# One scale per block of 256 columns of the three input matrices, from the sum of all squares: top-k attention with a maxout layer

## Chip, cores and metric

The kernel runs on one core of a Trainium2 chip. The metric is the device time of one execution in microseconds (us). The time before is 1222.91 us, the median of three runs (1222.42 to 1224.28).

## Reference

Attention over 8 batches with 8 heads, 576 positions and 64 columns a head keeps in each row of scores the 32 largest and takes the softmax of these alone. The rows of all heads, 512 wide, then go through a maxout layer: the largest of three products with 512 x 768 matrices, and a product with a 768 x 512 matrix.

```python
scores = scale * np.matmul(q, k.transpose(0, 1, 3, 2))
kth = np.partition(scores, -top_k, axis=-1)[..., -top_k:-top_k + 1]
scores = np.where(scores >= kth, scores, -1000000000.0)
...
attn = attn / (np.sum(attn, axis=-1, keepdims=True) + 1e-09)
x = np.matmul(attn, v)
...
h = np.maximum(np.maximum(x @ w1, x @ w2), x @ w3)
return h @ w_out
```

Inputs and output are float32; the kernel gets the weights as the low and high words of 64-bit numbers.

## The kernel before

**Attention.** A unit is a batch, one pair of heads and one or two blocks of 128 rows; the last 64 rows of two pairs of heads make one unit of their own. TensorE multiplies q and k (qk, L469), ScalarE brings the scores to SBUF (evac, L477), VectorE finds the largest of seven stretches of each row (sweep, L486) and from them a pivot; ScalarE marks what lies above the pivot (sign, L526), GpSimd multiplies (window, L531), VectorE takes the eight largest of the rest and picks the 32nd (below, L535, and pick), and masks the row (mask, L574). ScalarE takes exponentials (expo, L583), TensorE transposes (turn, L629 to L634), ScalarE copies these to SBUF (turned, L642), and TensorE multiplies by the values (values, L659). VectorE scales the result (scaled_x, L676), and ScalarE and GpSimd split it into two float16 parts.

**The maxout layer.** Per batch there are two parts, 256 and 320 columns wide. For each of the six blocks of 128 rows of the inner width and each of the three matrices TensorE makes twelve float16 matmuls (layer, L716: high times high, low times high, high times low, over four blocks). largest (L723, L725) brings the first product out of PSUM on ScalarE and folds the second and third into it on VectorE, each multiplied by the value rises of that matrix and block. ScalarE and GpSimd split the result (L728, L731), and TensorE multiplies by the output matrix (layer2, L776).

**The weights.** Each of the three input matrices is cut into three blocks of 256 columns (CUT), which makes nine jobs, in the order of blocks, the three matrices of a block one after the other. For each job SP loads (load_job), VectorE decodes the words into float32 in three instructions (decode, L261 to L263) and ScalarE squares (square_w, L272). TensorE then adds the squares of each column by four matmuls with a matrix of bfloat16 ones (sum_w, L279), VectorE takes the largest column (column_scale, L289), and powers (L185 to L189) makes of its exponent a power of two for scaling down and one for scaling back. After the third matrix of a block common_scale (L297 to L299) finds the largest of the three and sets rises, the factors that bring the three products to one scale. cut (L323, L326, L329) scales the weights of a job by that job's own factor on ScalarE and splits them into two float16 parts on ScalarE and GpSimd, half a job at a time. The output matrix comes in six jobs with one scale from the sum of all squares, which the square's accumulator gives (norm_scale, L200 to L208, with matmuls by float32 ones), and rows_scale (L305 to L308) joins it to the scales of the blocks.

**The order.** All of this is put down as pieces, each with an engine, an estimated cost, what it needs, the rings of buffers that it takes, and a rank: the number of the unit in the sequence plus an offset from the table OFFSETS (L41) by kind of piece. The pieces of the weights have ranks D0 to D3 (load, decode, square, sum, scale) and C0 to C3 (cut). in_order (L67) runs through time: for each engine, SP among them, it takes among the pieces whose rank lies within LEAD of the lowest the first that can begin within PATIENCE of the earliest. On TensorE it stays with pieces of the same kind for up to STICK ns, as changes between matmuls of different row or column groups have prices (SWITCH). The maxout layer is a filling: its pieces are taken in their own order where TensorE would otherwise be idle. What comes out is the order of each engine's queue, and each queue runs in order. Decoding shares a port with GpSimd, so pieces marked alone keep GpSimd's pieces away.

**Lines that the change touches.** OFFSETS, STICK, LEAD and PATIENCE; ones_b (L225), square_w, sum_w, column_scale, common_scale, scaled in cut, the loop of weights (L352 to L398), and the two evacuations in largest.

Of the kernel before, what the change touches and what calls it, by code (L numbers as in the profile page):

```python
# [8 lines left out]
F32 = mybir.dt.float32  # L9
F32R = mybir.dt.float32r  # L10
F16 = mybir.dt.float16
BF16 = mybir.dt.bfloat16
I32 = mybir.dt.int32
# [21 lines left out]
STICK = 131.6  # L35
WINDOW = 150
LEAD = 122.4
# [3 lines left out]
OFFSETS = {'C0': -71.38, 'C1': 6.04, 'C2': 17.6, 'C3': 26.23, 'D0': -1.46, 'D1': -8.59, 'D2': 13.79, 'D3': 20.14, 'E00': -5.21, 'E01': 4.78, 'E02': -0.01, 'E10': -0.7, 'E11': -11.12, 'E12': 11.25, 'N': -1.35, 'Pl': 20.57, 'R': 10.18, 'S': -2.96, 'T00': -16.7, 'T01': 27.24, 'T02': -10.92, 'T10': 34.43, 'T11': -25.56, 'T12': 24.01, 'U': -1.7, 'U0': -40.97, 'V': -4.3, 'V0': -88.25, 'Y': 6.38, 'Z': -8.84, '_E00': -50.75, '_E01': -3.75, '_E02': 10.74, '_E10': -47.5, '_E11': 8.93, '_E12': -45.31, '_N': -3.33, '_Pl': -99.0, '_T00': -57.59, '_T01': -22.38, '_T02': -27.69, '_T10': -82.8, '_T11': 11.41, '_T12': -5.44, '_Y': -57.77, '_Z': 21.36, '_d0': 3.39, '_d1': 0.48, '_e00': -27.05, '_e01': -112.55, '_e10': 3.08, '_e11': -97.31, '_g0': -67.77, '_g1': -48.33, '_g2': -97.9, '_g3': -19.67, '_h0': -0.67, '_h1': 5.89, '_h2': -4.11, '_k0': -60.14, '_k1': -24.36, '_k2': 1.73, '_k3': 5.68, '_m0': -59.82, '_m1': -51.76, '_m2': -40.28, '_m3': 0.62, '_p1': 3.43, '_p2': 3.94, '_p3': 5.7, '_p4': -60.33, '_p5': -1.94, '_q0': 1.95, '_q1': 2.38, '_r0': -70.22, '_r1': 4.68, '_s00': 0.7, '_s01': 4.86, '_s10': -42.03, '_s11': 3.25, '_v': 6.42, '_w0': -27.73, '_w1': -88.17, '_w2': -37.74, '_w3': -19.46, '_x0': 4.4, '_x1': 11.43, '_x2': 12.29, '_x3': 11.43, '_y': -77.91, '_z0': 11.5, '_z1': 11.06, 'd0': 7.71, 'd1': -21.2, 'e00': -0.07, 'e01': -0.48, 'e10': 7.08, 'e11': 4.86, 'g0': 1.51, 'g1': -17.65, 'g2': -8.45, 'g3': -2.84, 'h0': -0.16, 'h1': 8.34, 'h2': 0.48, 'k0': 1.66, 'k1': -16.87, 'k2': -0.51, 'k3': -15.62, 'm0': -10.99, 'm1': -11.53, 'm2': 9.41, 'm3': -0.62, 'p1': 8.83, 'p2': 6.51, 'p3': -17.58, 'p4': -10.41, 'p5': 7.85, 'q0': -2.71, 'q1': -1.91, 'r0': 1.52, 'r1': -11.44, 's00': 7.12, 's01': 8.27, 's10': 2.02, 's11': 6.61, 'v': 37.68, 'w0': 12.22, 'w1': -30.53, 'w2': -77.46, 'w3': -66.95, 'x0': 9.89, 'x1': 11.8, 'x2': 13.05, 'x3': -3.87, 'y': -12.65, 'z0': 3.14, 'z1': 5.24}  # L41
# [107 lines left out]
PATIENCE = {'PE': 127.1, 'DVE': 125.5, 'ACT': 0.0, 'POOL': 12.8, 'SP': 0.0}  # L149
# [3 lines left out]
def kernel(ctx, tc, q, k, v, moe_w1, moe_w2, moe_w3, moe_w_out, out):  # L153
# [71 lines left out]
    ones_b = const.tile([P, P], BF16, name="ones_b")  # L225
    nc.vector.memset(ones_b, 1.0)
    columns = {}
# [37 lines left out]
    squares_of = {}  # L265

    def square_w(j):

        at0, n = place(j)
        squares = squares_of[j] = wk.tile([P, JOB], BF16, name="junk", bufs=2)  # L270
        kw = dict(accum_out=wosq[:, j - 3 * NB:j - 3 * NB + 1]) if j >= 3 * NB else {}
        nc.scalar.activation(squares[:, :n], wall[:, at0:at0 + n], AF.Square, **kw)  # L272

    def sum_w(j):

        columns[j] = ps_m.tile([P, 512], F32, name="m")
        squares = squares_of.pop(j)
        for c in range(KC):
            nc.tensor.matmul(columns[j][:, :CUT], ones_b, squares[:, c * CUT:(c + 1) * CUT], start=(c == 0), stop=(c == KC - 1))  # L279
# [5 lines left out]
    def column_scale(j):  # L285
# [5 lines left out]
        if i == 2:  # L291
            common_scale(cb)
# [812 lines left out]
```

## Time and profile before

| | us |
|---|---|
| median of three runs | 1222.91 |
| the profiled execution | 1222.68 |
| its span, first to last instruction | 1220.9 |
| TensorE busy | 1137.3 |
| VectorE busy | 1104.6 |
| ScalarE busy | 1031.5 |
| GpSimd busy | 545.9 |

The mean clock granted to TensorE is 0.959 of full speed. Busy times are of one execution; the busy time of TensorE holds modelled ends of matmuls, so that a short pause between two of them may not show. The names of engines in the rows are PE (TensorE), PEld (its weight loads), DVE (VectorE), ACT (ScalarE), POOL (GpSimd) and SP (SyncE).

### The profile page before, as it was taken

How to read it: one execution, taken by the hardware profiler on the slowest of the kernel's cores; microseconds unless marked ns; L12 is line 12 of the kernel's file. 1: busy time of each engine (PE TensorE's matmuls, PEld its weight loads, DVE VectorE, ACT ScalarE, POOL GpSimd, SP SyncE). 2: the span in 40 equal slices, each digit the busy share in tenths (PEclk: the TensorE clock that was granted, in tenths of full speed). 3: DMA queues.
4: the chain of work that ended last, by engine and by line, in shares of the span. 5: the costliest groups of instructions: out<-in, count | busy, mean ns of one | idle time of the engine just before them, and what ended most of it. 6: DMA issues, size and time to landing. Idle time of an engine off the chain costs nothing.

```text
span 1220.9 us, 27377 instructions
## 1 busy us (share of the span) xinstructions
PE 1137.3 (93%) x8817; PEld 776.7 (64%) x8817; DVE 1104.6 (90%) x5413; ACT 1031.5 (84%) x2692; POOL 545.9 (45%) x503
## 2 busy tenths in 40 slices
PE   5367968999899999999999999999999999999998
PEld 2234844675676767666776767666776757666765
DVE  7999999999999999999899999999899999999311
ACT  5699979999989998988889998898899989889411
POOL 2354734445443544543544544543444544546110
PEclk8577977999899999999999999999999999999999
DMA  6232111211011102020111102020111100000000
GB/s 243 86 128 87 55 57 39 62 32 49 32 31 49 32 20 68 10 71 1 49 31 49 32 29 60 10 71 2 49 32 49 32 30 19 10 10 1 19 18 29
DMA packets 25751, 54.39 MB, mean 45 GB/s; under 512 B 2688, under 2 KB 2944, under 8 KB 25600
## 3 DMA queue, kind: packets, MB, share of 16 engines
q1 hardware_dynamic: 25296, 52.14, 13.1%
q8 instruction: 71, 1.16, 0.4%
q14 instruction: 80, 0.66, 0.2%
q10 hardware_dynamic: 304, 0.43, 0.1%
HBM read 43.12 MB, written 9.44 MB: 43 GB/s over the span
## 4 chain that ended last, share of the span: by engine, by line
PE 44%; DVE 36%; ACT 13%; POOL 4%; issue 3%; DMA 0%; POOLq 0%; ACTq 0%; DVEq 0%
PE m L716 18%; DVE L L486 8%; DVE ssb L574 8%; PE tr L659 8%; PE s L469 6%; PE m L776 6%; DVE Q L535 6%; PE tr L634 5%; POOL w L531 4%; ACT w L526 3%; ACT pm L583 3%; DVE h L725 3%; ACT pT L642 2%; DVE nR L510 2%; ACT ssb L477 1%
## 5 line engine op out<-in xcount | busy, mean ns | idle before, releaser
L531 POOL TENSOR_TENSOR w<-ssb,w 128x576 f32<-128x576 f32 x288 | 400.1, 1412 | 289.1 <-ACT w L526 259.5
L716 PE MATMUL m<-xh,wall 128*128 128x256 f16 (+1 forms) x2304 | 433.6, 286 | 1.3 <-DVE h L725 1.0
L716 PEld LDWEIGHTS <-wall 128*128 128x128 f16 x3456 | 337.3, 98 | 86.1 <-issue 10.4
L716 PE MATMUL m<-xl,wall 128*128 128x320 f16 (+1 forms) x1152 | 329.3, 286 | 0.1
L486 DVE MAX8 L<-ssb 128x8 f32<-128x82 f32 (+1 forms) x2016 | 311.9, 229 | 5.6 <-ACT ssb L477 5.6
L583 ACT ACTIVATE pm<-ssb,nb 128x576 f32<-128x576 f32 x288 | 223.4, 776 | 55.0 <-DVE ssb L574 54.7
L574 DVE SCALAR_TENSOR_TENSOR ssb<-ssb,kth 128x576 f32<-128x576 f32 x288 | 230.3, 832 | 2.4
L642 ACT COPY pT<-tr 128x512 f32<-128x512 f32 (+1 forms) x432 | 216.6, 514 | 14.4 <-PE tr L631 6.8
L526 ACT ACTIVATE w<-ssb,Q 128x576 f32<-128x576 f32 x288 | 223.5, 777 | 5.6 <-DVE Q L518 5.4
L535 DVE MAX8 Q<-w 128x8 f32<-128x576 f32 x288 | 214.2, 751 | 14.4 <-POOL w L531 13.0
L469 PE MATMUL s<-qk 64*128 64x288 f32 (+1 forms) x1280 | 191.6, 449 | 13.8 <-ACT ssb L477 8.8
L634 PE MATMUL tr<-ident,pm 128*128 128x128 f32 x1152 | 180.3, 283 | 22.9 <-ACT pm L583 11.6
L477 ACT ACTIVATE ssb<-s 128x576 f32<-128x576 f32 x288 | 184.9, 654 | 12.6 <-PE s L469 12.5
L659 PE MATMUL tr<-pT,vt 128*64 128x256 f32 (+1 forms) x1920 | 185.8, 345 | 0.0
L634 PEld LDWEIGHTS tr<-ident,pm 128*128 128x128 f32 x1152 | 131.6, 143 | 75.2 <-ACT pm L583 21.0
L659 PEld LDWEIGHTS tr<-pT,vt 128*64 128x64 f32 x1920 | 112.3, 143 | 71.3 <-issue 19.1
L469 PEld LDWEIGHTS s<-qk 64*128 64x128 f32 (+1 forms) x1280 | 99.9, 184 | 79.1 <-ACT ssb L477 29.2
L725 DVE SCALAR_TENSOR_TENSOR h<-m,rises,h 128x256 f32<-128x256 f32 (+1 forms) x192 | 97.3, 507 | 52.2 <-PE m L716 51.7
L731 POOL TENSOR_TENSOR hl<-h,hh 128x256 f16<-128x256 f32 (+1 forms) x96 | 70.4, 733 | 159.4 <-ACT hh L728 80.0
L776 PE MATMUL m<-wall,hh 128*128 128x512 f16 (+1 forms) x444 | 130.5, 376 | 0.6 <-POOL wall L329 0.6
L683 POOL TENSOR_TENSOR xl<-xs,xh 128x256 f16<-128x256 f32 (+1 forms) x80 | 50.0, 625 | 141.2 <-ACT xh L679 41.7
L776 PE MATMUL m<-wall,hl 128*128 128x512 f16 (+1 forms) x222 | 83.4, 376 | 0.0
(95 smaller groups left out, 1092.4 us busy)
## 6 DMA issues: line engine op xcount, KB each, us to landing
vt<-in_v_dram SPq DMA_DIRECT2D x32, 320.0 KB, 3.3
qk<-in_k_dram SPq DMA_DIRECT2D x34, 288.0 KB, 3.3
qk<-in_q_dram SPq DMA_DIRECT2D x33, 288.0 KB, 3.6
wall<-in_moe_w_dram SPq DMA_DIRECT2D x16, 512.0 KB, 4.5
out_dram<-ob SPq DMA_DIRECT2D x32, 256.0 KB, 2.0
wall<-in_moe_w_out_dram SPq DMA_DIRECT2D x3, 512.0 KB, 3.9
ssb<-in_moe_w_out_dram SPq DMA_DIRECT2D x3, 512.0 KB, 3.6
wall<-in_moe_w_dram SPq DMA_DIRECT2D x4, 256.0 KB, 6.8
```

What stands on the lines that cost most here:

```text
L469: nc.tensor.matmul(to[:, h, :HALF], both[sl, 0, c0:c0 + m], both[sl, 1, i * HALF:(i + 1) * HALF], start=True, stop=True)
L486: nc.vector.max(d["L"][:, t, k, :], d["ssb"][t][:, EDGES[k]:EDGES[k + 1]])
L526: nc.scalar.activation(d["w"][t], d["ssb"][t], AF.Sign, bias=d["Q"][:, t, 0:1], scale=-1.0, accum_out=d["cnt"][:, t:t + 1])
L531: return nc.gpsimd.tensor_tensor(d["w"][t], d["ssb"][t], d["w"][t], ALU.mult)
L535: nc.vector.max(d["Q"][:, t, 1:NW], d["w"].pop(t))
L574: return nc.vector.scalar_tensor_tensor(ss, ss, d["kth"][:, t:t + 1], ss, ALU.is_lt, ALU.subtract, accum_out=d["lost"][:, t:t + 1])
L583: nc.scalar.activation(d["pm", t // 2][:, t % 2], d["ssb"][t], AF.Exp, bias=d["nb"][:, t:t + 1], scale=-1.0 / SHRINK, accum_out=d["sums"][ ...
L634: nc.tensor.transpose(pt[:, j * P:(j + 1) * P], pm[:, i, 64 * i + j * P:64 * i + (j + 1) * P], ident)
L642: nc.scalar.copy(pT[:, 512 * i:512 * i + m] if i < 2 else pT[:, 8 * P:10 * P], pt[:, :m])
L659: nc.tensor.matmul(to, vt[:, block if i < 4 else 8 + h, :], keys, start=(i == 0), stop=(i == 4))
L716: nc.tensor.matmul(box["ps", i][:, :c1 - c0], a, bb[:, kc, c0:c1], start=(kc == 0 and k == 0), stop=(kc == KC - 1 and k == 2))
L776: nc.tensor.matmul(box["po"][:n, :ds.stop - ds.start], a[:, f, cs], columns_of(bb, ds), start=(f == 0 and k == 0), stop=(f == FC - 1 and k ...
```

## The change

One scale per block of 256 columns takes the place of one for each matrix and block. The square of a job adds up its rows by the accumulator into a column of wisq. After the third matrix of a block three float32 matmuls of one column with the float32 ones add these three columns over the partitions and over the matrices, and powers makes the block's power of two from that sum, straight from PSUM. The three products of a block then have one scale, so rises goes, and the evacuations in largest multiply by the constant H_SCALE. ones_b, the column sums, column_scale and common_scale go. A job's cut needs the scale of its block. The estimated costs of the changed pieces are new, and so are all offsets, STICK, LEAD and PATIENCE. The diff, with the table of offsets cut:

```diff
--- before.py
+++ after.py
@@ -32,13 +32,13 @@
 SWITCH = {(None, None): 0.0, (None, 'rows'): 205.0, (None, 'columns'): 230.0, ('rows', None): 96.0, ('rows', 'rows'): 0.0,
           ('rows', 'columns'): 96.0, ('columns', None): 78.0, ('columns', 'rows'): 78.0, ('columns', 'columns'): 0.0}
 AHEAD_OF_FILL = 6
-STICK = 131.6
+STICK = 198.9
 WINDOW = 150
-LEAD = 122.4
+LEAD = 126.3
 SLACK = 2000.0
 LOCK_A = -144.0
 LOCK_B = -103.0
-OFFSETS = {
...
+OFFSETS = {
...
 LATE = {'PE': 102.0, 'DVE': 60.0, 'ACT': 95.0, 'POOL': 10.0, 'SP': 2000.0}
 
 
@@ -146,7 +146,7 @@
 DECODE_OUT = 1920.0
 LOAD_JOB = 6500
 SCORES = 960
-PATIENCE = {'PE': 127.1, 'DVE': 125.5, 'ACT': 0.0, 'POOL': 12.8, 'SP': 0.0}
+PATIENCE = {'PE': 167.4, 'DVE': 126.9, 'ACT': 7.4, 'POOL': 5.9, 'SP': 0.0}
 
 
 @with_exitstack
@@ -222,9 +222,7 @@
     jobs = [(i, cb) for cb in range(NB) for i in range(3)]
     w_in = (moe_w1, moe_w2, moe_w3)
     wosq = const.tile([P, FC], F32, name="wosq")
-    ones_b = const.tile([P, P], BF16, name="ones_b")
-    nc.vector.memset(ones_b, 1.0)
-    columns = {}
+    wisq = const.tile([P, 3 * NB], F32, name="wisq")
     raw_of = {}
 
     def halves(i, c, c0, n):
@@ -262,41 +260,25 @@
         nc.vector.scalar_tensor_tensor(w, low, 29, w, ALU.logical_shift_right, ALU.bitwise_or)
         return nc.vector.scalar_tensor_tensor(w, top, -0x40000000, w, ALU.bitwise_and, ALU.bitwise_or)
 
-    squares_of = {}
-
     def square_w(j):
 
         at0, n = place(j)
-        squares = squares_of[j] = wk.tile([P, JOB], BF16, name="junk", bufs=2)
-        kw = dict(accum_out=wosq[:, j - 3 * NB:j - 3 * NB + 1]) if j >= 3 * NB else {}
-        nc.scalar.activation(squares[:, :n], wall[:, at0:at0 + n], AF.Square, **kw)
-
-    def sum_w(j):
-
-        columns[j] = ps_m.tile([P, 512], F32, name="m")
-        squares = squares_of.pop(j)
-        for c in range(KC):
-            nc.tensor.matmul(columns[j][:, :CUT], ones_b, squares[:, c * CUT:(c + 1) * CUT], start=(c == 0), stop=(c == KC - 1))
-
-    backs = const.tile([P, NB, 3], F32, name="backs")
-    rises = const.tile([P, NB, 3], F32, name="rises")
+        squares = wk.tile([P, JOB], BF16, name="junk", bufs=2)
+        to = wosq[:, j - 3 * NB:j - 3 * NB + 1] if j >= 3 * NB else wisq[:, j:j + 1]
+        nc.scalar.activation(squares[:, :n], wall[:, at0:at0 + n], AF.Square, accum_out=to)
+
+    def sum_w(cb):
+
+        total = totals[cb] = ps_m.tile([P, 512], F32, name="m")
+        for i in range(3):
+            nc.tensor.matmul(total[:, 0:1], ones, wisq[:, 3 * cb + i:3 * cb + i + 1], start=(i == 0), stop=(i == 2))
+
+    totals = {}
     tops = const.tile([P, NB], F32, name="tops")
 
-    def column_scale(j):
-
-        i, cb = jobs[j]
-        m2 = sm.tile([P, 1], F32, name="m2", bufs=1)
-        nc.vector.tensor_reduce(m2, columns.pop(j)[:, :CUT], AX.X, ALU.max)
-        powers(f"w{j}", m2, const, backs[:, cb, i:i + 1])
-        if i == 2:
-            common_scale(cb)
-
-    def common_scale(cb):
-
-        down = sm.tile([P, 1], F32, name="down_wi")
-        nc.vector.tensor_reduce(tops[:, cb:cb + 1], backs[:, cb], AX.X, ALU.max)
-        nc.vector.tensor_scalar(down.bitcast(I32), tops.bitcast(I32)[:, cb:cb + 1], -1.0, float(254 << 23), ALU.mult, ALU.add)
-        nc.vector.tensor_scalar(rises[:, cb], backs[:, cb], down, H_SCALE, ALU.mult, ALU.mult)
+    def block_scale(cb):
+
+        powers(f"w{cb}", totals.pop(cb)[:, 0:1], const, tops[:, cb:cb + 1])
 
     def rows_scale():
 
@@ -318,7 +300,7 @@
         box = {}
 
         def scaled():
-            down = scale_of[f"w{j}"][0] if j < 3 * NB else scale_of["rows"][:, (j - 3 * NB) * P // CUT:(j - 3 * NB) * P // CUT + 1]
+            down = scale_of[f"w{jobs[j][1]}"][0] if j < 3 * NB else scale_of["rows"][:, (j - 3 * NB) * P // CUT:(j - 3 * NB) * P // CUT + 1]
             box["ws"] = io.tile([P, 2 * CUT], F32, name="ws", bufs=2).rearrange("p (c n) -> p c n", n=CUT)
             nc.scalar.activation(box["ws"], w, AF.Copy, scale=down)
 
@@ -351,7 +333,7 @@
 
     def weights():
 
-        decoded, loads, scales = {}, {}, {}
+        decoded, loads, scales, summed = {}, {}, {}, []
         last = None
         for j in range(3 * NB + FC):
             mine = j < 3 * NB
@@ -371,19 +353,22 @@
                 last = piece("DVE", DECODE_IN if mine else DECODE_OUT, lambda j=j, part=part: decode(j, part), [loads[j], *([last] if last else [])], rank, alone=True)
             decoded[j] = last
             free.append(last)
-            y = piece("ACT", 1000 if mine else 570, lambda j=j: square_w(j), [last], rank, [("junk", rel)])
-            if mine:
+            y = piece("ACT", 1180 if mine else 760, lambda j=j: square_w(j), [last], rank, [("junk", rel)])
+            rel.append(y)
+            if not mine:
+                scales.setdefault("wo", []).append(y)
+                continue
+            cb = jobs[j][1]
+            summed.append(y)
+            if len(summed) == 3:
                 release = []
-                z = piece("PE", 4 * 110, lambda j=j: sum_w(j), [y], rank, [("m", release)])
+                z = piece("PE", 3 * 70, lambda cb=cb: sum_w(cb), summed, rank, [("m", release)])
                 z.slack = SLACK / 4
-                rel.append(z)
-                scales[j] = piece("DVE", 640 if jobs[j][0] < 2 else 900, lambda j=j: column_scale(j), [z], rank)
-                release.append(scales[j])
-            else:
-                rel.append(y)
-                scales.setdefault("wo", []).append(y)
+                scales[cb] = piece("DVE", 460, lambda cb=cb: block_scale(cb), [z], rank)
+                release.append(scales[cb])
+                summed = []
         wo = scale_pieces(norm_scale("wo", lambda: wosq, const), scales["wo"], (0.0, "D3"))
-        wo = piece("DVE", 280, rows_scale, [wo, *(scales[j] for j in range(3 * NB))], (0.0, "D3"))
+        wo = piece("DVE", 280, rows_scale, [wo, *(scales[cb] for cb in range(NB))], (0.0, "D3"))
         wo_scaled.append(wo)
         for j in range(3 * NB + FC):
             mine = j < 3 * NB
@@ -391,7 +376,7 @@
             for part in range(KC // 2 if mine else 1):
                 f = cut(j, part)
                 rel = []
-                a = piece("ACT", 580, f[0], [scales[j] if mine else wo], cutting, [("ws", rel)])
+                a = piece("ACT", 580, f[0], [scales[jobs[j][1]] if mine else wo], cutting, [("ws", rel)])
                 h = piece("ACT", 530, f[1], [a], cutting)
                 lo = piece("POOL", 1130, f[2], [h], cutting)
                 rel.append(lo)
@@ -720,9 +705,9 @@
             ps, prev = box.pop(("ps", i)), box.get("h")
             h1 = box["h"] = wk.tile([P, WIDE], F32, name="h1", bufs=3)
             if i == 0:
-                nc.scalar.activation(h1[:, :w], ps[:, :w], AF.Copy, scale=rises[:, f * P // CUT, 0:1])
+                nc.scalar.activation(h1[:, :w], ps[:, :w], AF.Copy, scale=H_SCALE)
             else:
-                nc.vector.scalar_tensor_tensor(h1[:, :w], ps[:, :w], rises[:, f * P // CUT, i:i + 1], prev[:, :w], ALU.mult, ALU.max)
+                nc.vector.scalar_tensor_tensor(h1[:, :w], ps[:, :w], H_SCALE, prev[:, :w], ALU.mult, ALU.max)
 
         def high_h(f, cs, w, box):
             nc.scalar.copy(H[0][:, f, cs], box["h"][:, :w])
```

## Rows read from the trace of the kernel before

**Rows 1.** The page, part 4: the chain that ended last, by engine.
```profile
PE 44%; DVE 36%; ACT 13%; POOL 4%; issue 3%; DMA 0%; POOLq 0%; ACTq 0%; DVEq 0%
```

**Rows 2.** Stretches: length; PE, PEld, DVE, ACT, POOL busy us; clock; DMA; GB/s.
```profile
0.00:30.00 30.00, 14.86 (x66) 6.90 (x66) 23.24 (x151) 17.75 (x37) 8.16 (x13) 0.82 0.71 247
30.00:60.00 30.00, 11.52 (x49) 6.88 (x49) 29.38 (x109) 19.66 (x46) 11.42 (x9) 0.56 0.24 76
60.00:120.00 60.00, 41.39 (x246) 23.04 (x245) 58.60 (x238) 57.12 (x133) 26.64 (x23) 0.77 0.32 108
120.00:150.00 30.00, 28.78 (x277) 23.99 (x277) 29.54 (x145) 27.64 (x73) 21.54 (x19) 1.00 0.21 72
150.00:210.00 60.00, 44.74 (x273) 26.82 (x273) 55.55 (x238) 49.75 (x129) 25.27 (x25) 0.77 0.12 39
210.00:300.00 90.00, 89.08 (x693) 58.93 (x685) 87.80 (x445) 88.29 (x239) 44.92 (x39) 1.00 0.17 52
300.00:1100.00 800.00, 792.89 (x6372) 550.29 (x6371) 772.98 (x3926) 718.53 (x1909) 378.79 (x345) 1.00 0.11 34
...
1148.00:1215.00 67.00, 67.00 (x493) 47.94 (x490) 12.50 (x28) 13.53 (x27) 8.43 (x12) 1.00 0.05 17
```

**Rows 3.** Timeline of VectorE, 58 to 63 us: start, length, instruction.
```profile
58.02 0.42 DVE L289 TENSOR_REDUCE m<-m 128x1 f32<-128x256 f32 x1
58.47 0.15 DVE L185 TENSOR_SCALAR e<-m 128x1 int32<-128x1 int32 x1
...
58.79 0.18 DVE L546 SCALAR_TENSOR_TENSOR oh<-spots,cnt 128x36 f32<-128x36 f32 x1
...
62.58 0.16 DVE L297 TENSOR_REDUCE tops<-backs 128x1 f32<-128x3 f32 x1
...
63.10 0.69 DVE L261 TENSOR_SCALAR wall<-wall 128x1024 int32<-128x1024 int32 x1
```

**Rows 4.** Groups by shape: squares (busy us, mean ns, idle before), and decodes by stretch.
```profile
L272 ACT ACTIVATE junk<-wall 128x1024 bf16<-128x1024 f32 x9 | 9.5, 1060 | 2.5 <-DVE wall L263 2.4
L272 ACT ACTIVATION_READ_ACCUMULATOR junk<-wall 128x1 f32 x6 | 1.2, 200 | 0.0
...
90.00:120.00 30.00, 3.68 (x3) 0.77 0.23 73
```

**Rows 5.** Groups by shape: the column sums, and single-column sums.
```profile
L279 PE MATMUL m<-junk,ones_b 128*128 128x256 bf16 x36 | 6.6, 319 | 17.3 <-ACT junk L272 17.3
L204 PE MATMUL tr<-s,ones 128*128 128x1 f32 x18 | 3.1, 243 | 1.7 <-DVE s L200 1.7
```

**Rows 6.** Scaling in cut (ns min/median/max, first and last start), and TensorE's first use.
```profile
L323 ACT ACTIVATE ws<-wall,down_w x18: 705/721/804, 48.5 to 133.1; 128x512 f32<-128x512 f32 x18
...
121.38 0.39 PE L716 MATMUL m<-xh,wall 128*128 128x256 f16 x2
```

**Rows 7.** Groups by shape: evacuations and instructions with and without a value per partition.
```profile
L642 ACT COPY pT<-tr 128x256 f32<-128x256 f32 x144 | 53.4, 377 | 7.1 <-PE tr L631 6.8
...
L725 DVE SCALAR_TENSOR_TENSOR h<-m,rises,h 128x256 f32<-128x256 f32 x96 | 45.4, 473 | 20.1 <-PE m L716 19.6 <-ACT w L526 0.2
...
L723 ACT ACTIVATE h<-m,rises 128x256 f32<-128x256 f32 x48 | 22.8, 475 | 2.4 <-PE m L716 2.2
...
L262 DVE SCALAR_TENSOR_TENSOR wall<-wall 128x1024 int32<-128x1024 int32 x9 | 11.0, 1226 | 0.3
...
L262 DVE SCALAR_TENSOR_TENSOR wall<-wall 128x512 int32<-128x512 int32 x3 | 2.1, 693 | 0.1
```

**Rows 8.** Waits of TensorE's weight loads, 300 to 1100 us: total us, times, longest.
```profile
PEld s L469 <- issue: 20.0, 74, 0.4
...
PEld tr L659 <- issue: 10.0, 31, 0.8
...
PEld tr L634 <- issue: 9.7, 25, 0.4
PEld L716 <- issue: 8.8, 24, 0.4
```

More of the change, by code (lines that the diff above doesn't have):

```diff
@@ new lines @@
+OFFSETS = {'C0': -85.08, 'C1': 10.84, 'C2': 17.46, 'C3': 25.77, 'D0': -31.26, 'D1': -15.51, 'D2': 13.13, 'D3': 19.32, 'E00': -6.12, 'E01': 3.36, 'E02': 2.71, 'E10': 1.6, 'E11': -0.98, 'E12': 11.85, 'N': -1.08, 'Pl': 15.72, 'R': 10.06, 'S': -1.5, 'T00': -33.76, 'T01': 6.79, 'T02': -4.0, 'T10': 21.71, 'T11': -56.23, 'T12': -49.7, 'U': -0.98, 'U0': -56.22, 'V': -7.76, 'V0': -82.86, 'Y': 8.22, 'Z': 11.55, '_E00': -52.62, '_E01': 3.79, '_E02': 11.53, '_E10': -34.89, '_E11': 8.66, '_E12': -32.8, '_N': -1.76, '_Pl': -93.83, '_T00': -85.49, '_T01': -62.11, '_T02': -77.61, '_T10': -88.94, '_T11': -3.51, '_T12': -51.06, '_Y': -54.87, '_Z': -11.77, '_d0': 4.75, '_d1': -15.85, '_e00': -33.89, '_e01': -38.38, '_e10': 2.77, '_e11': -71.91, '_g0': -114.12, '_g1': -107.02, '_g2': -91.53, '_g3': -76.25, '_h0': 1.34, '_h1': -87.65, '_h2': 3.46, '_k0': -5.19, '_k1': -12.81, '_k2': -34.04, '_k3': 6.33, '_m0': -91.2, '_m1': -61.8, '_m2': -50.18, '_m3': -3.41, '_p1': 1.21, '_p2': -10.05, '_p3': 4.5, '_p4': -89.28, '_p5': 0.72, '_q0': 2.16, '_q1': 3.68, '_r0': -24.57, '_r1': 4.0, '_s00': 0.5, '_s01': 4.74, '_s10': -46.66, '_s11': 3.59, '_v': -24.96, '_w0': -25.56, '_w1': -106.84, '_w2': -51.56, '_w3': -89.38, '_x0': 4.88, '_x1': -10.43, '_x2': 12.22, '_x3': 11.14, '_y': -102.99, '_z0': 11.25, '_z1': 10.79, 'd0': 6.65, 'd1': -10.23, 'e00': 0.19, 'e01': 5.39, 'e10': 7.99, 'e11': 5.37, 'g0': -1.98, 'g1': -0.63, 'g2': -8.13, 'g3': -5.27, 'h0': 0.18, 'h1': 8.72, 'h2': 2.16, 'k0': 1.44, 'k1': -17.66, 'k2': -3.96, 'k3': -11.02, 'm0': -10.37, 'm1': -11.19, 'm2': 9.69, 'm3': 1.66, 'p1': 8.83, 'p2': 6.74, 'p3': -15.9, 'p4': -9.63, 'p5': 8.01, 'q0': -0.44, 'q1': 0.64, 'r0': -2.6, 'r1': -11.6, 's00': 7.05, 's01': 8.28, 's10': 1.64, 's11': 6.31, 'v': 9.29, 'w0': -62.27, 'w1': -8.55, 'w2': -35.78, 'w3': -3.71, 'x0': 9.61, 'x1': 13.9, 'x2': 8.83, 'x3': -1.92, 'y': -12.29, 'z0': 6.21, 'z1': 3.6}
```

1 line of the change is left out of this document (removed).

## Prediction

> **What bounds the kernel now.** I read the chain of waits first. It ends on TensorE for 44% of the span and on VectorE for 36% [rows 1], so two engines carry the end and the stages have to be told apart. The table of stretches does that [rows 2]. Up to 210 us VectorE is busy for 196.3 us (the sum of five rows), and most of its idle time lies in the first 30 us, where the first scores are still on their way. TensorE is busy for 141.3 us there and idle for 68.7 us. In this first stage, attention of batch 0 and the decoding of the weights share VectorE, and whatever VectorE does not do in it, the rest does earlier. From 210 us TensorE is busy 89.1 of 90, then 792.9 of 800, and in the end 67.0 of 67 us: the multilayer part that had piled up fills every gap. VectorE stands close behind in the long stretch (773.0 of 800), ScalarE further back (718.5). In the last 67 us VectorE has 12.5 us of work. So the end is: the point at which TensorE becomes full, plus TensorE's remaining work, which the change does not lessen. A microsecond of VectorE saved before 210 us counts nearly in full, unless ScalarE takes over there: between 60 and 120 us it is busy 57.1 of 60. A microsecond of VectorE saved after 210 us counts only where TensorE waits for it.
>
> One profiled execution took 1222.68 us with a span of 1220.9, so 1.8 us lie around the span. The median of the runs is 1222.91, 0.2 us above. I set the sum against 1222.9. A measurement can tell about 0.2% (2.4 us) from no change.
>
> **Scales on VectorE, removed.** For each of nine jobs VectorE runs a maximum over 256 columns and three small operations; start to start this takes from 58.02 to 58.79, 0.77 us [rows 3]. Per block three more operations follow, 62.58 to 63.10, 0.52 us. Together 9 x 0.77 + 3 x 0.52 = 8.5 us. What stays is the three small operations of powers(), once per block: from 58.47 to 58.79, 0.32 us, now read from PSUM as they would be then; 3 x 0.32 = 1.0 us. VectorE is relieved of 7.5 us, all in the first stage. The memset of the bfloat16 ones is gone too, at nothing: it lies in the start, before the first scores come.
>
> **Squares on ScalarE, lengthened.** The nine squares of the input matrices now add up their rows. The same line already does this for the six squares of the output matrix, where a read of the accumulator of 200 ns follows; the square of 1024 takes 1060 ns itself [rows 4]. So 9 x 0.2 = 1.8 us on ScalarE; by the decodes, three in every 30 us from 30 us on, six of these lie between 60 and 120 us, where ScalarE has 2.9 us idle [rows 2, 4]. Bounds: nothing, if the order moves other ScalarE work to the stretch from 150 to 210 us (10.3 us idle there), and 1.8 us if all of it is on the path. I take 1.8, the row of the stretch where most of them stand.
>
> **Sums on TensorE.** 36 matmuls of 256 columns go, 6.6 us of busy time, and 9 single-column ones come, at 0.24 us each some 2.2 us [rows 5]. TensorE is idle for 68.7 us of this stage, so I take nothing for it, in either direction. If that cover were gone it would give back about 4 us. The wait in TensorE's queue is of more interest: five times it stood before a sum, 17.3 us together, until the squares were there [rows 5], with the score products and transposes of attention queued behind it, and evacuations on ScalarE and the searches on VectorE behind those. There are three sums now, each needing three squares. VectorE was nearly full all the same, so these waits were covered and taking them away gives nothing more; where a new sum stood badly, three waits of the old mean of 3.5 us, 10 us, would again have to get past the same cover. I take zero.
>
> **Later cuts.** A job could be scaled once its own scale was there, the first at 48.5 us [rows 6]; now it waits for the third matrix of its block, 62.6 us by the old order [rows 3]. TensorE first needs cut weights at 121.4 us [rows 6], so blocks 0 and 1 have tens of microseconds to spare. In the last block all six cuts, not four, can come after the last scale. That is two more scalings of 0.72 us with their casts and differences, some 3 us at worst on ScalarE before the last third of the first multilayer part. The old order ran until 133.1 us with them and TensorE had idle time behind that, between 150 and 210 us. Nothing is taken; up to 3 us stay in the bound above.
>
> **The constant in the maxima.** largest() now multiplies by a constant in place of a value per partition. On ScalarE the evacuation of 256 columns by such a value takes 475 ns and a plain copy of 256 columns from PSUM 377 [rows 7]: 98 ns less, 96 times, 9.4 us. On VectorE the nearest pair is the decode, with constants: 693 ns at 512 and 1226 at 1024 give 1.04 ns a column and 160 ns fixed. The maximum at 256 takes 473 ns, of which 1.04 x 256 leave 206. So about 47 ns less, 192 times, 9.0 us; the other bound is nothing, if the fixed part comes from PSUM and not from the value. Twelve of the 192 lie before 210 us and about 24 in the last stretch, so 156 x 47 ns = 7.3 us of VectorE fall where the two engines run side by side. TensorE is full there, so this mostly becomes idle time of VectorE. TensorE's in-order queue does stop there for results of ScalarE and VectorE, though never for long, and shorter producers take some of that. Bounds 0 and 7.3 us; I take 2, nearer the lower end, because TensorE's row (792.9 of 800) leaves 7 us in all.
>
> **The order.** Every offset, the readiness to stick to a kind of matmul (131.6 to 198.9 ns) and the patience of TensorE (127.1 to 167.4) change. Each piece keeps its instructions and each load its bytes, but loads on SP and pieces on all queues move by up to a unit against each other. No row prices an order that hasn't run. The nearest is the idle time of TensorE's weight loads that the profile calls issue, at changes of kind: 154 gaps, 48.5 us, 0.31 us each in 800 us [rows 8]. A tenth fewer or more is 5 us either way. I take zero and keep both ends.
>
> **Sum.** -7.5 + 1.8 - 2 = -7.7 us: 1222.9 - 7.7 = 1215.2 us.
>
> **Rivals.**
> ScalarE binds at once. It is 95% busy from 60 to 120 us; of its 2.9 us of idle time six accumulator reads take 1.2, and if no other work moves away, the stage gets shorter by 1.7 us only and VectorE idles. Time 1221.2, no change by the bound. Against it: ScalarE has room on both sides of this stretch, and the order is redone. Chance 0.14.
>
> VectorE binds throughout. A busy share of TensorE need not mean that it is at its limit, since ends are modelled and pauses of 0.3 us at each change of kind hide behind them; the 154 gaps [rows 8] could be grouped away if VectorE were not late, and VectorE's 773.0 of 800 us is the real limit. Then 7.3 us count in full beside 7.5: 1222.9 - 14.8 = 1208.1 us. Against it: TensorE's queue is back to back in the last 67 us and the same work is only a little looser before. Chance 0.20. The Trainium skill, Perfetto Trace Analysis, section Identifying the Most-Contended Engine, says that matmul busy time is no good measure of nearness to the limit while for VectorE occupancy is; by that rule VectorE is the engine to relieve, and this is the case it would make. The trace can't decide it beforehand, as both stand above 96%.
>
> TensorE's kind changes get dearer, and the kernel slower. Place: 210 to 1148 us, in TensorE's in-order queue, where the new constants let it hold out 67 ns longer for a piece of the same kind. If the producer is late, everything behind waits. Price: 154 gaps x 938/800 = 181, times 67 ns = 12.1 us, against the first stage's 5.7: 1222.9 - 5.7 + 12.1 = 1229.3 us. It eats the gain of 7.7 when a gap grows by 43 ns on average, and shows as slower from 56 ns. For it: TensorE has almost no idle time to absorb a worse order. Against it: sticking should also make the changes fewer. Chance 0.19.
>
> That the change does not do what it says: the constant saves nothing on VectorE because the fixed part belongs to PSUM. Then about 2 us of the sum are lost and 1217.2 us remain; it lies inside the forecast's case.
>
> **How the numbers follow.** Forecast 0.47, around 1215.2 with 1210 to 1219 by its own bounds (first stage -7.5 to -2.7, long stretch 0 to -7.3, not both at their ends). Faster by over 0.2% is the forecast and the VectorE rival: 0.67. Within 0.2% is the ScalarE rival: 0.14. Slower is 0.19. The range goes from 1204 (the VectorE rival with an order some 4 us better) to 1227, which takes in the ScalarE rival and the lower half of the slower one.
>
> **What would show it.** Right: nine column maxima and their bookkeeping gone, three short groups in their place; 15 accumulator reads behind the squares; TensorE full by about 204 us instead of 210; evacuations near 375 and maxima near 425 ns at 256 columns; TensorE's busy time in the long stretch unchanged and VectorE's lower. Wrong: ScalarE at 58 or more of 60 with VectorE waiting for it between 60 and 120 us (first rival); a batch's period shorter by over a microsecond (second); more or longer issue gaps (third). An attention stage that ends much earlier or later than 6 us before the old one would upset the sum.

## The result and the profile after

The changed kernel takes 1211.61 us (median of four runs, 1211.44 to 1211.91); the kernel before took 1223.56 us beside it (median of four). The ratio is 0.9903, with a 95% interval from 0.9886 to 0.9921. That is 11.9 us less; 7.7 were forecast. The profiled execution took 1211.44 us with a span of 1209.7 us. Differences below are worked out from the ratios, times 1223 us, since the runs of before moved between 1222.9 and 1223.8 us from chip to chip.

First, where the scales are made now: the timeline of VectorE in the changed kernel around 63 us (start, length, instruction), the whole of what one block's scale costs there.

```profile
63.04 0.15 DVE L185 TENSOR_SCALAR e<-m 128x1 int32<-128x1 int32 x1
63.23 0.15 DVE L188 TENSOR_SCALAR down_w<-e 128x1 int32<-128x1 int32 x1
63.30 0.14 DVE L189 TENSOR_SCALAR tops<-e 128x1 int32<-128x1 int32 x1
63.36 0.81 DVE L559 SCALAR_TENSOR_TENSOR ssb<-ssb,kth 128x576 f32<-128x576 f32 x1
```

From 63.04 to 63.36 that is 0.32 us, three times in all, in place of the 8.5 us that [rows 3] lead to. Next, the groups by shape that answer to [rows 4, 5, 7] (busy us, mean ns, idle before):

```profile
L268 ACT ACTIVATION_READ_ACCUMULATOR junk<-wall 128x1 f32 x15 | 2.9, 196 | 0.0
...
L274 PE MATMUL m<-wisq,ones 128*128 128x1 f32 x18 | 2.4, 243 | 0.4 <-ACT junk L268 0.4
...
L710 DVE SCALAR_TENSOR_TENSOR h<-m,h 128x256 f32<-128x256 f32 x96 | 39.6, 413 | 27.9 <-PE m L701 27.3
...
L710 DVE SCALAR_TENSOR_TENSOR h<-m,h 128x320 f32<-128x320 f32 x96 | 45.9, 479 | 34.5 <-PE m L701 34.5
...
L708 ACT ACTIVATE h<-m 128x256 f32<-128x256 f32 x48 | 18.3, 381 | 3.0 <-PE m L701 2.9
```

The maximum at 256 columns went from 473 to 413 ns and the evacuation from 475 to 381: a value per partition costs VectorE 60 ns and ScalarE 94 ns. The nine further accumulator reads are there (15 in place of six), and the wait of TensorE for squares fell from 17.3 us to 0.4.

Then the table of stretches of the changed kernel (columns as in [rows 2]):

```profile
0.00:30.00 30.00, 18.22 (x80) 8.89 (x80) 23.06 (x149) 20.57 (x43) 8.00 (x13) 0.89 0.72 247
30.00:60.00 30.00, 16.69 (x91) 9.36 (x92) 27.86 (x107) 21.77 (x57) 9.79 (x8) 0.60 0.21 70
60.00:120.00 60.00, 30.25 (x153) 16.99 (x154) 58.42 (x245) 54.24 (x128) 29.91 (x26) 0.66 0.27 92
120.00:150.00 30.00, 25.86 (x230) 20.06 (x226) 29.23 (x121) 26.29 (x71) 17.24 (x17) 0.94 0.31 111
150.00:210.00 60.00, 45.77 (x353) 29.96 (x353) 55.80 (x258) 53.38 (x138) 29.64 (x30) 0.96 0.18 60
210.00:300.00 90.00, 88.60 (x668) 59.24 (x669) 87.56 (x445) 87.44 (x239) 46.55 (x41) 0.97 0.10 34
300.00:1100.00 800.00, 795.12 (x6447) 558.25 (x6446) 775.58 (x3993) 730.88 (x1959) 389.49 (x353) 1.00 0.11 34
```

TensorE's busy time in the long stretch hardly moved (792.9 to 795.1 of 800 us), but the number of matmuls in it did: 6372 before, 6447 after. That is 75 more in the same 800 us, some 9 us of work at the mean of 800/6372 = 0.126 us. The two kernels have different orders, so the mix differs a little: 16 fewer of these matmuls belong to the maxout layer's first products, 91 more to the rest. With that caveat, the greater part of the gain lies where the prediction had put its smaller term, and busy time doesn't show it. Runs below that share an order compare like with like. This count of matmuls, by stretch, is the measure that the experiments are read with. (The chain of waits of the changed kernel breaks off after 14% of the span, so it isn't compared with [rows 1].)

### The profile page after: what moved, and what is told of

Read it like the earlier page. It is cut to its first block, busy times and chain, and to the rows that moved or that the text cites. A ratio compares the mean times of both kernels' runs of the same rounds, so it can differ in the third digit from the quotient of the medians.

```text
span 1209.7 us, 27286 instructions
## 1 busy us (share of the span) xinstructions
PE 1124.4 (93%) x8799; PEld 776.0 (64%) x8799; DVE 1083.8 (90%) x5376; ACT 1025.4 (85%) x2701; POOL 547.4 (45%) x503
## 5 line engine op out<-in xcount | busy, mean ns | idle before, releaser
L559 DVE SCALAR_TENSOR_TENSOR ssb<-ssb,kth 128x576 f32<-128x576 f32 x288 | 234.7, 842 | 2.2
L710 DVE SCALAR_TENSOR_TENSOR h<-m,h 128x256 f32<-128x256 f32 (+1 forms) x192 | 85.6, 446 | 62.4 <-PE m L701 61.7
```

Of the source, the lines that this page charges most:

```text
L559: return nc.vector.scalar_tensor_tensor(ss, ss, d["kth"][:, t:t + 1], ss, ALU.is_lt, ALU.subtract, accum_out=d["lost"][:, t:t + 1])
```

## The experiments

Three theories: A, the forecast (VectorE's relief in the first stage counts nearly in full, the constant little); B, the new order made the gain; C, VectorE binds throughout. The kernels take the change apart three ways: the scales' arithmetic, the constant in the maxima, the order. In all but one of them one part is put in or taken out with the order of the queues kept.

### In the old order

**The scales alone.** Pieces and order of the kernel before; only what they run is changed:

```diff
-        squares = squares_of[j] = wk.tile([P, JOB], BF16, name="junk", bufs=2)
-        kw = dict(accum_out=wosq[...]) if j >= 3 * NB else {}
+        squares = wk.tile([P, JOB], BF16, name="junk", bufs=2)
+        kw = dict(accum_out=wosq[...] if j >= 3 * NB else wisq[:, j:j + 1])
...
+        if i < 2:
+            return
-            nc.tensor.matmul(columns[j][:, :CUT], ones_b, squares[...], ...)
+            nc.tensor.matmul(columns[j][:, 0:1], ones, wisq[:, 3 * cb + c:3 * cb + c + 1], ...)
...
+        if i < 2:
+            scale_of[f"w{j}"] = fixed, None
+        else:
+            powers(f"w{j}", columns.pop(j)[:, 0:1], const, tops[:, cb:cb + 1])
```

> The kernel before with the new scale arithmetic alone, its order of queues and the values per partition in the maxima kept; two of the three jobs of a block are cut by a fixed scale, so that no cut has to wait, and the bookkeeping of the three scales is left out. Theory A (the forecast: VectorE's relief in the first stage counts nearly in full): 5 to 7 us faster, TensorE full some 6 us earlier. Theory B (the new order made the gain, in the long stretch): 0 to 2 us faster, VectorE idle longer in the first stage. Theory C (VectorE binds throughout): 7.5 us faster.

Measured: 1220.87 us, ratio 0.9980 (0.9971 to 0.9989), 2.4 us less (1.3 to 3.5 by the interval). That is close to theory B's 0 to 2, and half or less of the 5 to 7 that A expected.

**The constant alone.**

```diff
-                nc.scalar.activation(h1[:, :w], ps[:, :w], AF.Copy, scale=rises[:, f * P // CUT, 0:1])
+                nc.scalar.activation(h1[:, :w], ps[:, :w], AF.Copy, scale=H_SCALE)
...
-                nc.vector.scalar_tensor_tensor(h1[:, :w], ps[:, :w], rises[:, f * P // CUT, i:i + 1], prev[:, :w], ALU.mult, ALU.max)
+                nc.vector.scalar_tensor_tensor(h1[:, :w], ps[:, :w], H_SCALE, prev[:, :w], ALU.mult, ALU.max)
```

> The kernel before with only the constant in the maxima in place of the value per partition; order kept, the relation of the three matrices' scales left out. Maxima at 256 columns 425 ns or less, evacuations near 377 ns in every theory. Theory A: 2 us faster. Theory B: 0 to 1 us faster. Theory C: 7 us faster.

Measured: 1216.50 us, ratio 0.9948 (0.9935 to 0.9962), 6.4 us less. That is near C's 7; A's 2 us lie outside the interval (4.6 to 8.0).

**Both**, still in the old order:

> Both edits of the two runs before in one kernel, order of queues of the kernel before kept. Theory A: 7 to 8 us faster than before, 4 us short of the changed kernel. Theory B: 0 to 3 us faster. Theory C: 12 us or more faster, as fast as the changed kernel or faster.

Measured: 1215.13 us, ratio 0.9932 (0.9918 to 0.9945), 8.3 us less. The two terms add up (2.4 + 6.4 = 8.8), and the total is what A forecast, for the wrong reasons.

**Which half of the constant?** One line of the diff of the constant each.

> The kernel before with the constant only in the 96 evacuations of the first product on ScalarE, some 90 ns shorter each (8.6 us in all); the 192 maxima on VectorE keep the value per partition. If VectorE is what limits the long stretch: 0 to 1.5 us faster. If ScalarE or the latency of its results is: 4 to 7 us faster, the larger part of what both constants gave (7 us).

Measured: 1222.03 us, ratio 0.9992 (0.9983 to 1.0001): no difference that can be told.

> The kernel before with the constant only in the 192 maxima on VectorE, some 60 ns shorter each (11.7 us in all, about 9.5 of it before the last stretch). If VectorE limits the long stretch: 5 to 7 us faster, the larger part of what both constants gave. If ScalarE does: 0 to 2 us faster.

Measured: 1216.62 us, ratio 0.9951 (0.9937 to 0.9964), 6.0 us less. Within the noise all of the constant's gain is VectorE's. That PSUM buffers come free earlier is a less likely cause: ScalarE's half frees the first product of every three 90 ns sooner and shows nothing. It is not excluded, as VectorE itself frees the other two.

**Is it ScalarE that keeps the scales' relief small in the old order?** Between 60 and 120 us it was the fuller engine of the run with the scales alone (58.22 of 60 us, VectorE 56.52), as the first rival had it. Next, the run without the accumulator reads. The rows of this stretch are those of the scales alone and of this run:

```profile
60.00:120.00 60.00, 41.53 (x239) 23.01 (x240) 56.52 (x218) 58.22 (x140) 26.69 (x24) 0.76 0.34 116
60.00:120.00 60.00, 39.69 (x239) 22.43 (x241) 57.30 (x223) 58.03 (x134) 26.89 (x24) 0.79 0.34 116
```

```diff
-        kw = dict(accum_out=wosq[...] if j >= 3 * NB else wisq[:, j:j + 1])
+        kw = dict(accum_out=wosq[...]) if j >= 3 * NB else {}
```

> The run with the scale arithmetic alone, old order, without the nine accumulator reads of ScalarE too (the block sums then add a fixed tile). If ScalarE takes over from VectorE in the first stage, where it was busy 58.2 of 60 us from 60 to 120 us in that run: 1 to 2 us faster than it, some 4.5 us faster than before. If something else holds the old order back (TensorE's waits, GpSimd): no change, 2 to 3 us faster than before.

Measured: 1220.86 us, ratio 0.9978 (0.9969 to 0.9987), the same as with the reads. So the reads aren't it. ScalarE is no less full without them (58.03 of 60 us), so the run does not free ScalarE, and whether ScalarE as such holds the stage back stays open.

The traces show one thing that takes part of the relief back. With the scales' arithmetic gone the decodes come at other times than the order was made for, and more of them meet a piece of GpSimd, which the planner had kept away. The decode that took 0.69 us at 63.10 in the kernel before [rows 3] now starts at 61.38, while a piece of GpSimd runs, and takes 1.61 us (run with the scales alone):

```profile
61.28 1.16 POOL L329 TENSOR_TENSOR wall<-ws,wall 128x512 f16<-128x512 f32 x1 [6.11 <-DVE e L185]
61.38 1.61 DVE L259 TENSOR_SCALAR wall<-wall 128x1024 int32<-128x1024 int32 x1
```

In the kernel before, the same piece of GpSimd ended at 63.07, just ahead of the decode. The group of these decodes, in the kernel before and with the scales alone:

```profile
L261 DVE TENSOR_SCALAR wall<-wall 128x1024 int32<-128x1024 int32 x9 | 6.9, 765 | 0.0
L259 DVE TENSOR_SCALAR wall<-wall 128x1024 int32<-128x1024 int32 x9 | 8.9, 994 | 0.0
```

Nine times 229 ns are 2.1 us. In all, VectorE's busy time over the whole run falls by only 3.7 us (1104.6 to 1100.9), where 7.5 had been worked out. The 2.4 us gained are about two thirds of these 3.7, as the constant's 6.4 are of its 9.6 (1104.6 to 1095.0). So in this order the scales count at about the same rate as the constant; it is the relief itself that came out smaller.

### In the new order

**A value per partition again**, in the changed kernel, holding the same constant:

```diff
+    rises = const.tile([P, NB, 3], F32, name="rises")
+    nc.vector.memset(rises, H_SCALE)
...
-                nc.vector.scalar_tensor_tensor(h1[:, :w], ps[:, :w], H_SCALE, prev[:, :w], ALU.mult, ALU.max)
+                nc.vector.scalar_tensor_tensor(h1[:, :w], ps[:, :w], rises[:, f * P // CUT, i:i + 1], prev[:, :w], ALU.mult, ALU.max)
```

> The changed kernel with its order kept, but with a value per partition (holding the same constant) in the maxima and evacuations again. Theory A: 2 us slower than the changed kernel, 1213.6. Theory B: 0 to 1 us slower. Theory C: 7 us slower, 1219.

Measured: 1217.75 us, ratio to before 0.9956 (0.9943 to 0.9970), 6.5 us slower than the changed kernel, as in the old order.

**VectorE's work on scales again**, on scratch:

```diff
         powers(f"w{cb}", totals.pop(cb)[:, 0:1], const, tops[:, cb:cb + 1])
+        for i in range(3):
+            nc.vector.tensor_reduce(spent[:, 0:1], load, AX.X, ALU.max)
+            if i < 2:
+                ...
+        nc.vector.tensor_reduce(spent[:, 4:5], load[:, 0:3], AX.X, ALU.max)
+        ...
```

> The changed kernel with its order kept and VectorE's removed work put back on scratch, 12 operations more per block behind each block's scale, 2.5 us each time. Theory A: 5 to 7.5 us slower than the changed kernel. Theory B: 0 to 2 us slower, as TensorE has room early on. Theory C: 7.5 us slower.

Its timeline of VectorE shows the first of the three lumps, of which the first and the last instruction and the next one stand here:

```profile
63.87 0.41 DVE L287 TENSOR_REDUCE spent<-load 128x1 f32<-128x256 f32 x1
...
66.09 0.23 DVE L295 TENSOR_SCALAR spent<-load,spent 128x3 f32<-128x3 f32 x1
66.23 0.81 DVE L573 SCALAR_TENSOR_TENSOR ssb<-ssb,kth 128x576 f32<-128x576 f32 x1
```

From 63.87 to 66.23 are 2.36 us, three times 7.1 us. Measured: 1219.52 us, ratio 0.9971 (0.9962 to 0.9980), 8.3 us slower than the changed kernel. In the new order the early relief counts in full; in the old one it was 2.4. The two are not quite alike. Here the decodes don't depend on the scale work (857 ns with it, 867 without), and VectorE's busy time changes by 5.9 us (1089.7 and 1083.8), not 3.7. The work also stands in three lumps, where the kernel before had most of it spread over nine jobs, and a lump holds up everything queued behind it. How much of the 8.3 us is due to that was not tested.

**Both again**, that is, the new order with the old durations:

> Both of the last two in one: the new order with the old durations. Theory A: 7 to 9 us slower than the changed kernel, close to 1220. Theory B: at most 3 us slower, so still 9 us faster than before by its order alone. Theory C: 14 us slower, so slower than before.

Measured: 1225.27 us, ratio 1.0018 (1.0009 to 1.0027): 2.2 us slower than before. Theory B falls: the order by itself gives nothing, as far as these lumps stand for the old work. (ScalarE's reads, the new sums and the later cuts stay in this run.)

**The new code with the old constants of the planner:**

```diff
-STICK = 198.9
+STICK = 131.6
...
-PATIENCE = {'PE': 167.4, 'DVE': 126.9, 'ACT': 7.4, 'POOL': 5.9, 'SP': 0.0}
+PATIENCE = {'PE': 127.1, 'DVE': 125.5, 'ACT': 0.0, 'POOL': 12.8, 'SP': 0.0}
```

> The changed kernel with the old table of offsets and the old STICK, LEAD and PATIENCE, so that the planner makes another order from the same pieces. Theory A: within 3 us of the run with both edits, 1215 us. Theory B: 1220 us or slower, as the old numbers were not made for these pieces. Theory C: about as fast as the changed kernel, 1212 us.

Measured: 1226.40 us, ratio 1.0024 (1.0013 to 1.0035), 15 us slower than the changed kernel from the same pieces. Other pieces with the old numbers give a third order, and a bad one: between 60 and 120 us VectorE is busy 50.2 us only. A set of offsets belongs to the pieces that it was made for.

### The two limits

**More work on TensorE**, in the kernel before:

```diff
+                if f == 0:
+                    nc.tensor.matmul(box["ps", i][:, :c1 - c0], halves(i, 0, 0, P)[0], xh[:, 0, c0:c1], start=True, stop=True)
```

> The kernel before with one more matmul ahead of each of the 48 products of the first block of each part (48 x about 0.123 us = 5.9 us of TensorE work, overwritten by the product itself). If TensorE is the limit from 210 us on (theories A and B): 5 to 6 us slower. If VectorE is (theory C): about 1 us slower, from the last stretch alone.

Measured: 1225.83 us, ratio 1.0023 (1.0014 to 1.0033), 2.8 us for 5.9 us of work. About half of it found room in a TensorE that was busy 99% of the stretch. Of VectorE's 9.4 us (156 maxima between 210 us and the last stretch x 60 ns) about two thirds counted, or 6.4 us with ScalarE's half and 6.0 without. So both engines limit, VectorE rather more, though the intervals (1.7 to 4.0 us for TensorE's work) leave the shares rough.

**A version that might beat both.** If VectorE limits, one more value per partition can go: the power of two of the values moves from scaled_x on VectorE into a copy on ScalarE (folded), for every unit but the first, whose power is not there yet at the copy.

```diff
+        if d["folded"]:
+            nc.scalar.activation(rsw, wide, AF.Copy, scale=vs_of[units[n][0]][0])
+        else:
+            nc.scalar.copy(rsw, wide)
...
-        nc.vector.scalar_tensor_tensor(x, xp, vs_of[b][0], d["pT"][:, 0:len(us), 9, :], ALU.mult, ALU.mult)
+        nc.vector.scalar_tensor_tensor(x, xp, 1.0 if d["folded"] else vs_of[b][0], d["pT"][:, 0:len(us), 9, :], ALU.mult, ALU.mult)
```

> The changed kernel with one more value per partition taken off VectorE: the power of two of the values goes into widen on ScalarE (a copy of 128 columns, now with a value per partition, 143 times), and scaled_x on VectorE multiplies by the constant 1. Order kept, result exact, as a power of two commutes. VectorE: 79 times 60 ns, 4.7 us less, some 4.3 of it ahead of the last stretch; ScalarE: 143 times about 90 ns, 13 us more. If VectorE limits the new order throughout and ScalarE has room, as the constants' two halves showed in the old order: 3 to 4.5 us faster than the changed kernel, 1207 to 1209. If ScalarE is close behind: no change, or up to 5 us slower. If TensorE limits: within 1 us.

Measured: 1210.97 us, ratio 0.9895 (0.9879 to 0.9912): the interval overlaps the changed kernel's almost wholly, so no gain is shown, though one of up to some 3 us is not excluded. The groups by shape say that the trade took place:

```profile
L592 ACT ACTIVATE rsw<-rs,down_v 128x128 f32<-128x128 f32 x142 | 55.6, 405 | 2.9 <-DVE rs L583 2.7
...
L667 DVE SCALAR_TENSOR_TENSOR xs<-tr,pT 128x256 f32<-128x256 f32 x63 | 26.0, 412 | 3.5 <-PE tr L650 3.5
```

VectorE's product fell from 473 ns in the kernel before to 412, and ScalarE's copy rose from 301 ns in the changed kernel to 405. 4.7 us off VectorE against some 15 us onto ScalarE (142 x 104 ns) come out about even.

### All of them in one view

The table of stretches once more, two rows a kernel, up to 300 us and from there to 1100. The first count after a busy time of TensorE is its matmuls. In order: before; scales alone; constant alone; both in the old order.

```profile
0.00:300.00 300.00, 230.36 (x1582) 146.56 (x1582) 284.11 (x1319) 260.20 (x649) 137.95 (x126) 0.85 0.25 84
```

```profile
0.00:300.00 300.00, 229.56 (x1582) 145.69 (x1584) 282.26 (x1299) 262.80 (x663) 138.02 (x126) 0.85 0.25 85
300.00:1100.00 800.00, 792.41 (x6373) 549.96 (x6370) 773.71 (x3930) 719.27 (x1913) 380.39 (x347) 1.00 0.11 33
```

```profile
0.00:300.00 300.00, 230.06 (x1584) 146.65 (x1584) 283.56 (x1319) 259.39 (x649) 138.08 (x126) 0.85 0.26 84
300.00:1100.00 800.00, 793.17 (x6416) 553.66 (x6414) 771.86 (x3959) 718.98 (x1928) 383.97 (x349) 1.00 0.11 34
```

```profile
0.00:300.00 300.00, 232.62 (x1578) 148.88 (x1580) 280.79 (x1295) 261.25 (x661) 137.84 (x126) 0.84 0.25 85
300.00:1100.00 800.00, 794.42 (x6417) 554.49 (x6415) 771.72 (x3962) 718.19 (x1928) 384.94 (x351) 1.00 0.11 33
```

In the new order: changed kernel; values per partition again; scale work again; both again.

```profile
0.00:300.00 300.00, 225.39 (x1569) 144.51 (x1570) 281.94 (x1315) 263.70 (x671) 141.13 (x128) 0.86 0.24 84
```

```profile
0.00:300.00 300.00, 224.80 (x1569) 145.08 (x1570) 283.16 (x1316) 264.88 (x671) 141.64 (x128) 0.85 0.25 84
300.00:1100.00 800.00, 793.46 (x6411) 554.43 (x6409) 778.46 (x3979) 733.26 (x1950) 386.20 (x351) 1.00 0.11 34
```

```profile
0.00:300.00 300.00, 220.04 (x1510) 141.80 (x1510) 279.51 (x1309) 255.86 (x648) 139.06 (x128) 0.84 0.25 84
300.00:1100.00 800.00, 795.16 (x6444) 557.38 (x6442) 777.06 (x4006) 732.68 (x1963) 386.01 (x351) 1.00 0.11 34
```

```profile
0.00:300.00 300.00, 218.78 (x1505) 140.25 (x1507) 279.87 (x1305) 256.54 (x644) 137.79 (x127) 0.84 0.25 84
300.00:1100.00 800.00, 793.66 (x6411) 553.65 (x6409) 778.85 (x3974) 734.71 (x1954) 386.36 (x351) 1.00 0.11 34
```

Up to 300 us the matmuls of the sums have to be taken off, 36 where columns are summed and 18 elsewhere. What is left against the kernel before (1546 and 6372):

| kernel | up to 300 us | 300 to 1100 us | x 0.126 us | measured, us |
|---|---|---|---|---|
| scales, old order | +18 | +1 | -2.4 | -2.4 |
| constant, old order | +2 | +44 | -5.8 | -6.4 |
| both, old order | +14 | +45 | -7.4 | -8.3 |
| changed kernel | +5 | +75 | -10.1 | -11.9 |
| values again, new order | +5 | +39 | -5.5 | -5.4 |
| scale work again, new order | -54 | +72 | -2.3 | -3.5 |
| both again, new order | -59 | +39 | +2.5 | +2.2 |

The counts follow the times within 2 us. (The matmuls are of different lengths. The totals, 8817 before and 8799 in the changed kernel, differ by just the 18 fewer sums, so none is missing on one side only.) Read by column: the constant adds 33 to 44 matmuls to the long stretch, in either order, and about nothing before it. The scales act before 300 us alone, by 12 to 18 matmuls in the old order and by 59 to 64 in the new. The new order is 28 to 39 matmuls ahead in the long stretch, but with the old durations it starts 59 behind; the scales' relief fills just that gap. From one order to the other these counts compare different mixes, so here they are rough.

A second measure has no such mix: VectorE masks 288 blocks of rows, a batch's worth being 36, and within one order the 72nd and the 288th mask are the same instructions. Both of the kernel before, then both of the changed kernel:

```profile
322.53 0.82 DVE L574 SCALAR_TENSOR_TENSOR ssb<-ssb,kth 128x576 f32<-128x576 f32 x1
1130.68 0.81 DVE L574 SCALAR_TENSOR_TENSOR ssb<-ssb,kth 128x576 f32<-128x576 f32 x1
...
316.73 0.80 DVE L559 SCALAR_TENSOR_TENSOR ssb<-ssb,kth 128x576 f32<-128x576 f32 x1
1109.64 0.81 DVE L559 SCALAR_TENSOR_TENSOR ssb<-ssb,kth 128x576 f32<-128x576 f32 x1
```

| kernel | 72nd mask at, us | from it to the 288th | from there to the end of the span |
|---|---|---|---|
| before | 322.5 | 808.2 | 90.2 |
| scales, old order | 319.6 | 808.5 | 90.4 |
| constant, old order | 321.6 | 802.8 | 90.2 |
| both, old order | 320.1 | 802.9 | 90.4 |
| changed kernel | 316.7 | 792.9 | 100.0 |
| values again, new order | 316.8 | 797.7 | 100.1 |
| scale work again, new order | 325.3 | 792.9 | 99.8 |
| both again, new order | 326.2 | 797.6 | 100.1 |

In either order the scales move the start alone, and the constant shortens the six batches alone, by about 5 us. Within an order the last column hardly moves, so the time follows the end of attention. The new order gets through the six batches some 10 us sooner, and leaves as much more of the maxout layer behind them.

## Why the prediction was right, and where not

It was right that the kernel gets faster, and the time lies in the range. The sum of 7.7 us was short of 11.9, and in the old order two of its terms had about each other's size. That their total comes near there (8.3 us) is luck: one was too large, the other too small. The 1211.6 us lie 3.6 below the forecast and 3.5 above the rival in which VectorE binds throughout, so the time alone does not choose between them; the runs do.

**Scales on VectorE (-7.5).** The work removed is as worked out: 0.32 us is left per block. That it counts nearly in full held in the new order (8.3 us when put back, in lumps) and not in the old (2.4), where slower decodes took 2.1 us of it back. The text had reckoned with the stage, not with the order in it.

**Squares (+1.8).** The reads are there, 196 ns each; taking them away made no difference that can be told in the old order. Their price on the path there is near the lower bound of zero, not the 1.8 that was taken. In the new order it was not tested.

**Sums and later cuts (0).** The single-column products stand in the rows as 18, two for each of the nine; their busy time, 2.4 us, is near the 2.2 that was said. The last cut of an input matrix starts at 156.0 us in place of 133.1, and the first part of the maxout layer at 132.9 in place of 121.4. TensorE did not get full by 204 us, the sign that the text had named; between 150 and 210 us it is busy 45.8 of 60 us (44.7 before). It makes the later start up before 300 us (+5 matmuls). By the 72nd mask the changed kernel is 5.8 us ahead, near the 6 us that the text had named, but not by its terms: the scales give 8.5 us there in the new order, which without them would be 2.7 us behind.

**The constant (-2).** This is the step that failed: "TensorE is full there, so this mostly becomes idle time of VectorE", with 2 taken "because TensorE's row (792.9 of 800) leaves 7 us in all". The durations were near (60 ns, where 47 was worked out; 94 on ScalarE at 256 columns for 98), but the time measured 6.4 us in the old order and 6.5 in the new, close to the upper bound of 7.3. The row's 7 us of idle time were no bound: with the constant alone, in the same order, 44 more matmuls went into the same busy time. Nor did VectorE go idle, as it would have to if TensorE were full: the 138 maxima there got some 8 us shorter in all, and its busy time fell by 1.1 us only (773.0 to 771.9). The rival in which VectorE binds throughout had this part right, with its argument that modelled ends hide pauses. The Trainium skill, Perfetto Trace Analysis, section Identifying the Most-Contended Engine, says that TensorE's matmul busy share is no good measure of how near a kernel is to its limit; these runs agree, as 792.9 and 793.2 us of busy time held 6372 and 6416 matmuls in the same order. The sign named for that rival came as well: from the 72nd mask to the 288th a batch takes 134.7 us before, 133.8 with the constant alone and 132.2 in the changed kernel, where most of the difference is the order's. That rival's 1208.1 us was nevertheless too low: neither term counted in full in the old order, and 5.9 us of added TensorE work cost 2.8.

**The order (0).** With old durations it is worth +2.2 us, with the new ones -3.5 (0.9903 against 0.9932, a difference near the width of the intervals). Both lie inside the 5 us either way that were kept for it. The slower rival did not come: the issue gaps of [rows 8] are 144 in the changed kernel with 45.6 us, where they were 154 with 48.5:

```profile
PEld s L454 <- issue: 22.8, 82, 0.4
...
PEld tr L619 <- issue: 8.9, 23, 0.4
PEld tr L644 <- issue: 8.7, 25, 0.4
...
PEld L701 <- issue: 5.2, 14, 0.4
```

The mean is 0.32 us, as before, so the waits at changes of kind did not grow.

**ScalarE binds at once.** In the old order the early relief came out near that rival's 1.7 us, and ScalarE was the fuller engine, but the run without its reads did not get faster, so its mechanism is not shown (nor excluded, as ScalarE stayed as full). In the new order it did not happen: ScalarE is busy 54.2 of 60 us there.

Open: what besides the slower decodes keeps VectorE's early relief small in the old order, how much of its full count in the new one is due to the lumps, why the new order gets through the batches sooner, and whether a better set of offsets for the old pieces exists. None of these was tried.

## What to carry to other kernels

Where two engines are both over 96% busy, don't let TensorE's busy share decide which one limits: count its matmuls in equal stretches with the order kept, and price a saving on the other engine at more than half of its size (here about two thirds of the busy time that it saved). An order made by a planner belongs to the durations that it was made for (even a piece that gets shorter can push others into each other, as the decodes here), so a change that brings both is taken apart four ways: each part alone, both, and the new order with the old durations. And before an operand is made a value per partition, look whether a constant would do; in instructions of 473 and 540 ns that was 60 ns, 192 times.

## What had not been expected

The value per partition costs VectorE 60 ns at 128 columns as at 320: scaled_x at 128 columns went from 341 ns in the kernel before to 278 with the power of two moved, at 256 from 473 to 412, and the maximum at 320 from 540 to 479. On ScalarE it was 94 ns at 256 columns (475 to 381), 85 at 320 (525 to 440) and 104 in the copy of 128 (301 to 405). The Trainium skill, ScalarE: Activation LUTs, section What ACT_TABLE_LOAD costs, gives about 93 ns for each such operand, which these rows bear out; for VectorE it is the runs here that say it.

Moving a small cost from VectorE to ScalarE showed no gain at a rate of three to one, though ScalarE is idle for 69 of the 800 us; and 8.6 us taken off ScalarE alone showed none either.
